# A decode block of attention and MLP: the same 2394 tasks in another issue order

## Chip, cores and metric

One core of one Trainium2 chip. The metric is device time in microseconds of one execution; medians of several executions are given.

## The reference, cut to what matters

Two layers, each an attention block over a cache and an MLP, with residuals and layer norms. Eight rows (one token each), 32 heads of 128, and the last 1024 of 4096 cached positions:

```python
W = min(4096, max(256, Sk // 4))                 # 1024
q = (layernorm(x) @ wq).reshape(B, 1, 32, 128)
scores = einsum("bhqd,bhkd->bhqk", q, k_cache[:, :, Sk - W:]) * Dh ** -0.5
x = x + softmax(scores) @ v_cache[:, :, Sk - W:] @ wo      # reshaped
x = x + gelu(layernorm(x) @ w1 + b1) @ w2 + b2
# ... the same four lines once more, with the same weights and the same cache
```

K and V of the window are 134 MB, and both layers need them. The kernel keeps part of them between a row's layers and loads 336 units of 512 KB (176 MB).

## The kernel before

The kernel builds a list of tasks and issues them in an order that a string gives. A task has an engine, a function, the tasks that it needs, and the buffers that it takes and gives back. Only legal orders pass: a task must have no unmet need, and a buffer must be free.

```python
    def emit(self):
        ...
        code, todo = iter(ORDER), list(self.tasks)
        while todo:
            k = value[next(code)]            # position in the list of tasks not yet issued
            ...
            t = todo.pop(k)
            assert not t.waits
            if t.take is not None:
                self.room[t.take] -= 1
                assert self.room[t.take] >= 0, t.take
            t.fn()
            ...
    plan = Plan({"unit": NUNIT, "s": 2, "qz": 2, "p": 1, "pv": 1, "o": 1, "ot": 2,
                 "c": 4, "C": 3, "rd": 4, "park": 2})
```

For each row and layer the 16 head pairs are cut into jobs; "7.1.8-12" is row 7, second layer, pairs 8 to 11. The tasks of a job, in order of need: *query* (PE; second layer), *expand* (DVE), *scores* (PE, one per pair; each gives its K unit back), *exponent* (ACT), *turn* (PE transposes), *place* (ACT), *totals* (PE) and *inverse* (DVE), *values* (PE, one per pair; each gives its V unit back), four *folds* and two *halves* (DVE), *gathered* (PE, two small matmuls), *finish* (DVE), and in the first layer *project* (PE) and *accrue* (DVE). When all jobs of a row's first layer are projected, its MLP runs (*sums*, *hidden*, *outer*), then its second layer's queries. A *load* (SP) takes a unit of 27.

"p" is the scratch, which exponent and folds share.

```python
    scr = state.tile([P, 512], BF16, name="scr")
    acc, parts = scr[:, 0:256].bitcast(FP32), scr[:, 256:512].rearrange("p (h d) -> p h d", h=2)
    ...
    def exponent(job):
        nc.scalar.activation(scr[:], job.s_ps[:], ACT.Exp, scale=QSCALE)    # takes "p", turn gives it back
    def fold(job, t):                                                        # takes "p", gathered gives it back
        ...
            nc.vector.scalar_tensor_tensor(out=acc, in0=o[:, t], scalar=mask[:, t:t + 1], in1=acc, ...)
```

"c" and "C" are small slots in a PSUM tile of 512 columns, c_ps.

The softmax here doesn't subtract the row's maximum and nothing guards it: scores larger than these inputs give would overflow.

Of the kernel before, what the change touches and what calls it, by code (L numbers as in the profile page):

```python
# [17 lines left out]
D = 640  # L18
H = 32
# [3 lines left out]
F = 1728  # L23
# [12 lines left out]
NOT = {}  # L36
WINDOWS = ("0:1a 0:1b 0:2a 0:2b", "1:0a 0:3a 0:3b", "1:0b 1:1a 0:4a 0:4b", "1:1b 0:5a 0:5b", "1:2a 1:2b 0:6a 0:6b",
           "1:3a 1:3b 0:7a 0:7b", "1:4a 1:4b", "1:5a 1:5b 1:6a 1:7a 1:6b 1:7b")
WINDOWS = [[(int(w[0]), int(w[2]), ord(w[3]) - 97) for w in x.split()] for x in WINDOWS]
WPOS = (("w1", -1), ("w2", -1), ("wo", 8))  # L40
NHC = 13
HALF = F - NHC * P
ORDER = (
    "I))%(z<&2/,@/-%)%9yxyxyxyxyx2.z*z,z,z,y`y`y`z),,(4y[%yZyZyZ)zIy[y[yYyZyZyZyZyZyYyY&-(y[y[y]z9/&yTyT)+*(&(yRyqy"
    "RypyRyRyRyRyRyRyjyj&yVyXyVyYyYyYyYyYyYyYyYyYy]y]y]y]y_y_ykykyk{.{.yWyWyZyVyTyfyf{&yYyY{8yYyU{6yMyWyWyWyWyVy[y^"
    "y[y]y]%y_yU$#yQyQ$##yNyNyNzfzfyGyHyHyHyHyJyGyIyKz]yKz[z[yHyGzY#yFyFyFyFyFyFyF#z^yFyF$yMyDyDyDzVzgyDzHzH%yCzQzF"
    "%yByBzCzCzZyDyBzIzWzW#ziyAyAz>z>z>z>yAyAyAz`#z:y@y@y@zHz<$yAz8z9zCz3zRzBy?z2##z4y>z3z3z3y>z2z1z.z0z6y>#-&$z+yN"
    "z;z/z:z-yNy:z,y:yLyLy~&6)#z#z#z#z#z#z)y6yzy}y`y|/y5y}y~y~y5#y|yuyuyzyzyzyYy4yByUyUyByBysyryryr+yRypyRyq,##yOy2"
    "y2y2y;y;y0y1y9#%$#&y,yXy,y,y,y,y+y<y<yVy<y+y/y/y-yHyHy+yGy7#$#y*y*y2yDyGy*y*yBy*yXy*y&y)y,y,y>yjy,y)y+y+y)y*y8"
    "y8y8yIyIyIy8y]yHy*y*y*y3y/y*y(y)y)y0#%%##y#y,y,##y4y4y4y4y*y*x|y)x}y(x|y<y<y.y&y#$y$zVy$y6x~y&x}y3x~y$y$y$y/x~"  # L50
    "zJzJzJy#y#y,y#y#y#y#x}x~x~x~z?%y$zLx}x|##x|xzxzxzx}z4xzxzz2z?xzxzxzxzz;z.xzxzxzxz##z4xyxyxxz1xxz#xxz?x~y}y}$xx"
    "z)xwyzxwxwyxyxyxyxz1xyxwyzz.#y{xvxvxvxvyqxvyp#ys#&yoxsylynxsxvyvyvxvxsxsxt2$yfyoxnxqxqxqxqy&%y_y_y_y_y_$&#%yZ%"
    "#&y]xzxiyXxiyXxxxxxiyUyUyUyUy2yTyTxiy/y/xvxvxjxu%)yKxh-+xfxfxdy%y?y>x~y=xmxm$%xkx{x{y1y1y1xcxcxcxcxcxhxfxcxqxc"
    "y+yHxpxpxe#xdy)xdy($+xjxjxxxj$x~xwxaxa#xfy3y3xwx`x_x_%xcx^x^xqxazbxlx`x^x_xlxlxlx_x_x_x_x_zUxxxgx_x^xezP##&xb("
    "xcxYxmxWy#xZxXx_#xhxTxgx]x]x]x]x]x]xYxY#xoxoxoxo%x]xXx^x[xjxjx]x]x]x[z6xSxW#%xWz1xUxVxVxVxV#xZx]xTxTxTz%yrxWxX"
    "ypy}%#z0xRxQxQxQxQxQxTxMxPyrxPydz#xPxPxPxPxP#y`yixO#y[ytxNxNxNxNxNxNyVyVyVxNxKyZxM#yfyRyRyRyRyTxLxPySyPxLyQyZ$"
    "yYxNyOxKygygygxKyU#yLxK#xIxIyHyHyHyHyHyL#>&.$xDxDxDxDyCyAxGyAy>yJxGxDxDxEy7y7xE&yBxDxDy6y?y6y6y67y5y5xUxCy7xTx"
    "ky1y5y5*#&xQy,y/x@x@-+x|x|-#xzx<y$y$y$y$xJxJxJxJx|xwxxx_x_#x;&xrxyxYxsx;x;x;xUxoxVxUxpx;xCxCx7xexBx:x:*xMxMx?x"
    "9x9$####xYx4x4x6x3x1x@x4x4x4x2x3x;x;x;xOx;x3x3xzx3x3x3x3xHx6xtx5x3x4x4x3xVxBxBxBx;xRxRxRxRx3x3x3x>x3x3x3##)x9x"
    ";x0x:$xC#x6z,x-x5x?x?#x4x1x2xKxKxK#x,x0x0x0x0x0x4x/%x3x3x.x2ynx2x.x*x:%x9x,x8&yex7x-x-x&x,x,x2yKx+x+x+yHyHx+yj"  # L60
    "x+x-x-x+x,yBx/x*x*x*x*x*x*yIy;x*x*y9yE#yU###x%y4x%y>yNx%#yLx&x&x*yIx$x$x$x$x$y*y*y2$y)y)y)y)x(y,y(y(x#x&y%%w~w"
    "~x#w~x~x~x~x~y,x~x~x~y)w~-<9y%w{w{$wzwzxu,wy*xxwxwywywywywywywyxoxixgxhxhx/xjx/x/x/x/9wwxd##$x]x`x`wqx_zsx_x)x"
    "^x;wsxSzmzm)#$)%$wmw|wmzdwozcwmwmxNwmwmwmxMx,wuwuxA)#$wjxExGxG$wiwixqwiwiwiwkwywkwlwlwlwlwix9wvwsx7wux6x,wgx2w"
    "jwjwjwgwgxWwowox+whwhx:x+x-wgwgwgx%x###wfw|x#wgwgwuw|wuwgx?wzwzwzwzx#wgw~w~wyx6w}wvwgwfwv##*+wbwbwb#wq##)wnwnw"
    "nw^w^w]w]wgy<w]wdw]w`wtw]yVwa#y4#wbwbwZwawawkwkwkwkw^yHw`y(y(w`w`w`w`w^w_#w]y=wbw]w]w`w]w_wbw^wYw[w[w^xoxow[xn"
    "y-w]%y+wZ#y:xlwYwYwYwYxhw[xew[x{wYwYwbwYxa#y*x`x`x`x`x`x`$xawWwXx_wXwWx]wWx[x[xYwYxbwW#xWxWxWxWxWwWwVxhxZ###%3"
    "wQwQxNwQxQxOxMxZwQxNwQwQxVwSwSwQwRwRwRwRwRxDxD#xAxAxAxAxAxFxAx=wcwcxBx>xBxBx;wQ&wPw`w`w`)w_w_(3#0&$x<x2x;x1x,x"
    "-x/x/#wkx-x-x-wHwEwiwix)wgwgwUwUx(wGwHwHwHwGwG#(#%wKwywZwCwCwCwCwCwFwTwTwTwGwjwAwBwEwOwBwBwCw{wLwCwKwCwCwCwHw_"
    "wCwG+wRwWyMwGwGwBwBwBwD-wKwQwQwQwKwCwCwCwCwCwCw[w[$wZwZ&##*$w?w:wDwF#y?wAw;wC$#w7wJwJw9wIx}x}x}w=w>w>w>w>wF#w="
    "w=wAw=wAwAwAw;w?w<wHxkxkwH&w;()w:w6w9w9w3w8w8w7xlw7xkw;w;w7w:w7w6w2w4w4#w4w4w4w6w4w4xjw3w3w3w3w5w3w4w3xRxDx`w3"  # L70
    "w1xrw2w2x[x@w2xKxX#xWw1w1w2w1w1w1w1w1#%x5x5#w.xIw.w.x1w0x8w.xSx/x/x/x/x/x/x1w/w/x/w.#x-x-x+w-$#x)x)w+x(w+x&x;x"
    "+#w*w*xHx#x#x(x%w-w,w*#w{w}w(x,w)x+w{w(w($.%+x#w#wkwkw|w#w#w#wowowowowowmwn*$,()#w/w/wfwjwjwGwGw/wfqq#wcwCwCpw"
    "`w`w`w`w`w+w+$#w<w<nw(w(oow7wSwMoow#w#&w2vnnnwHnw-w-wE(#pw=lolnnlmmw9#(#rrrw3w5##hw2hhwDwDhhhhkkw*hvwQw(hiwNwN"
    "h%&&ueoeeow.eneew*w*nhejkll#ettiw1w1#rhhhegggcekkehdhh#c#oooeeeebjjbb_%#x+]]cccf]bb]]]#_wx_[#wuwuZZx(ZZZZ$#wmw"
    "mwmwzZZ^wj$]wiwiwrWWZWYWwlYwyWWw`whWXwf#w]w]w]w]w]VVV#)XwVwewZwXTTTTwUwRTTwRwRwRTwNwPwPwNwOwSTTTT%$$$$#)wD__MM"
    "MwBwBOO)Lw>MMUmw6UUw7UUMMwDMMMM(#$a^^w)JKw(w*w*]]u[KqrvvsuuZZw%ZKmppMKnLLL%###%DDw*MM#ZcccDDD]%CCCEGCDREESSSEE"
    "x1EB````OMDDDDKKKKJCGRRRDQGGGwq%#EBKKJDCCCCECDABDDBCA##$wW>>>>>wRwcwR@@wP>>>w[w[>wLwY###wI<wT<wHwHwH##::99wW:;"
    "wH$wSw?w?w?w?wE8w>w>88#7w<w:777w9788w6w6w68w:8888%)#)wvw*w+w+w+w+%/#)w&^^[[AA000r22(o;1/l08j0wV0-wU555FF/////]"
    "A[[[[00RRW0Q#(##$PPPO999LL#$&`$))F&((0CB0A0(((<(((99#)*&))333))))</--9...-)$($&(>(#&&&#88%%%@?F%J%%2E;(:1%#$$-"
    "-;$$$$$-$3#0&(++%+#*)$##$#")  # L80


class Job:
# [59 lines left out]
def _kernel(ctx: ExitStack, tc: tile.TileContext, A_small, A_k, A_v, A_wq, A_wo, B_w1, B_w2, out):  # L143
# [46 lines left out]
    xn = single["yT"]  # L190
# [67 lines left out]
    def narrow(n, nb, name):  # L258
        if nb == 1:
            return single[name]  # L260
        return units[free.pop()][:, 0:n * nb].rearrange("p (f b) -> p f b", b=nb)
# [464 lines left out]
    rows = []  # L726
    for b in range(NB):
        at, h = {}, (held | set(ALSO.get(b, ()))) - set(NOT.get(b, ()))
# [58 lines left out]
                         after=[d for d, h0, h1 in ends if h0 < h + 2 and h1 > h] + [head], take="park" if h == 0 else None)  # L787
            head = head or t

    jobs = rows[0][0]["s"] + rows[0][0]["k"]  # L790
    for b in range(NB):
        for layer, row, k in WINDOWS[b]:
            jobs = jobs + [rows[row][layer]["s"][k]]
        jobs = jobs + [job for job in rows[b][1]["k"] if any((w, i) not in job.held for w in "kv" for i in range(job.i0, job.i1))]
        jobs = jobs + (rows[b + 1][0]["k"] if b + 1 < NB else [])
# [7 lines left out]
    extra = {}  # L803
    for name, pos in WPOS:
        if pos < 0:
# [5 lines left out]
    def part0(job, last):  # L811
        def tail(done, h0, h1):
            projects(job, done, h0, h1, CHAIN, h1 == 2 * job.i1)
        add_job(job, (), 0, tail=tail if last else False)

    def part1(job, last, early, rank0, ask=None):
        job.ends = []
        done = add_job(job, early, rank0, ask=ask, tail=(lambda *x: job.ends.append(x)) if last else False)
        if not last:
            job.ends.append((done, 2 * job.i0, 2 * job.i1))  # L820

    for job in rows[0][0]["s"]:
        part0(job, False)
    for job in rows[0][0]["k"]:
        part0(job, job is rows[0][0]["k"][-1])
    for b in range(NB):
        ask = chain(b, projected[b] + asked + [weights["w1"], weights["w2"]])
        asked.clear()
        ahead = rows[b + 1][0]["k"] if b + 1 < NB else [rows[r][i]["s"][k] for i, r, k in WINDOWS[b]]
        base = min(t.pos for x in ahead for t in x.loads.values())  # L830
# [4 lines left out]
        for job in rows[b][1]["s"]:  # L835
            job.stored = ask(job, base, True)
        for layer, row, k in WINDOWS[b]:
            job = rows[row][layer]["s"][k]
            if layer == 0:
                part0(job, False)  # L840
            else:
                if b + 1 == NB:
                    job.direct = asked[:1]
                part1(job, b + 1 == NB and (layer, row, k) == WINDOWS[b][-1], [job.stored], 0)
        if b + 1 < NB:
# [11 lines left out]
    y8 = narrow(NKC, NB, "y8")  # L857
# [43 lines left out]
```

## Time and profile before

| | before |
|---|---|
| median (3 runs) | 490.17 us (490.11 to 490.87) |
| span of the profiled run | 488.7 us |
| PE / DVE / ACT busy | 80% / 52% / 16% |
| bytes moved | 192.20 MB |
| plateau of the loads | 416 to 420 GB/s |
| last landing, then first step of the last MLP, then end | 469.0, 478.1, 488.7 us |

The prediction below shows the lines. They are read in this order: the DMA and GB/s rows say that the stream of loads is full nearly everywhere (DMA at 9 in 37 of 40 slices, 416 to 420 GB/s in most); the stretches say where it isn't; the chain says what ends last.

### The profile page before, as it was taken

Reading aid. Unit: us, or ns where it says so; the run is one execution under the profiler, and the core shown is the slowest. Engines: PE = TensorE matmul, PEld = TensorE weight load, DVE = VectorE, ACT = ScalarE, POOL = GpSimd, SP = SyncE. Lnnn points to the kernel's source line nnn. Section 1 sums busy time; section 2 is a strip of 40 time slices with the busy share of each in tenths; the row PEclk is TensorE's granted clock in tenths of the full one; section 3 lists DMA queues with packets and bytes.
Section 4 is the critical chain, followed back from the end, with each engine's and each line's share of the span. In section 5 each row is a group of like instructions: output and inputs, shape, how many; then the busy total and the mean of one; then the engine's idle time right before and its main releaser. Section 6 shows DMA issues by size and latency. Waiting matters only on the chain.

```text
span 488.7 us, 16784 instructions
## 1 busy us (share of the span) xinstructions
PE 392.6 (80%) x7201; PEld 212.3 (43%) x7201; DVE 256.2 (52%) x1116; ACT 76.4 (16%) x195; POOL 12.7 (3%) x24
## 2 busy tenths in 40 slices
PE   1412645998899998898989989988999899889985
PEld 0300124553365436542564355535552464365354
DVE  3001422455735764477454755666466746757563
ACT  1000000111211111112111211112112111121220
POOL 1000000000000000000000000000000000000001
PEclk9996555556655755557555575587556655765765
DMA  8999999999999999999999999999999999999920
GB/s 328 417 420 420 438 421 417 418 417 418 416 418 415 416 416 420 402 411 419 418 380 403 417 417 411 412 419 414 416 416 417 418 373 392 416 415 414 417 91 4
DMA packets 49898, 192.20 MB, mean 393 GB/s; under 512 B 5792, under 2 KB 5792, under 8 KB 48800
## 3 DMA queue, kind: packets, MB, share of 16 engines
q1 hardware_dynamic: 49824, 191.13, 96.5%
q8 instruction: 56, 0.92, 0.7%
q14 instruction: 18, 0.15, 0.1%
HBM read 191.10 MB, written 0.01 MB: 391 GB/s over the span
## 4 chain that ended last, share of the span: by engine, by line
PE 53%; DMA 21%; DVE 17%; issue 4%; ACT 3%; POOLq 0%; ACTq 0%; SPq 0%; DVEq 0%
PE s_ps L435 13%; PE o_ps L476 12%; DMA unit<-in_A_k_dram 9%; PE c_ps L536 6%; PE c_ps L698 6%; DMA unit<-in_A_v_dram 6%; DVE scr L486 5%; DMA wo_sb<-in_A_wo_dram 4%; PE c_ps L450 3%; PE c_ps L319 3%; PE o_ps L511 2%; PE c_ps L359 2%; PE c_ps L500 2%; DVE scr L484 2%; PE c_ps L273 1%
## 5 line engine op out<-in xcount | busy, mean ns | idle before, releaser
L435 PE MATMUL s_ps<-unit,low 128*1 128x512 bf16 (+3 forms) x1024 | 123.5, 564 | 18.9 <-DMA unit<-in_A_k_dram 13.2
L476 PE MATMUL o_ps<-unit,misc 128*8 128x512 bf16 (+3 forms) x888 | 108.2, 555 | 12.9 <-DMA unit<-in_A_v_dram 6.8
L444 ACT ACTIVATE scr<-s_ps 128x512 bf16<-128x512 f32 x80 | 47.8, 597 | 217.7 <-PE c_ps L500 127.9
L486 DVE SCALAR_TENSOR_TENSOR scr<-o_ps,low,scr 128x128 f32<-128x128 f32 x213 | 74.1, 348 | 5.9
L484 DVE TENSOR_SCALAR scr<-o_ps,low 128x128 f32<-128x128 f32 x71 | 24.7, 348 | 46.7 <-PE c_ps L450 30.1
L536 PEld LDWEIGHTS <-wo_sb 128*128 128x128 bf16 x1280 | 38.4, 103 | 21.5 <-issue 14.3
L435 PEld LDWEIGHTS <-low 128*1 128x1 bf16 (+3 forms) x1024 | 22.6, 91 | 50.3 <-issue 34.8
L698 PEld LDWEIGHTS <-wq_sb 128*128 128x128 bf16 x1280 | 38.0, 102 | 13.4 <-issue 12.6
L698 PE MATMUL c_ps<-low,wq_sb 128*128 128x1 bf16 x1280 | 40.8, 165 | 0.8 <-ACT misc L454 0.4
L454 ACT CAST misc<-c_ps 128x48 bf16<-128x48 f32 (+2 forms) x80 | 21.8, 272 | 123.0 <-DVE misc L465 22.1
L476 PEld LDWEIGHTS <-misc 128*8 128x8 bf16 (+3 forms) x888 | 20.2, 91 | 38.6 <-issue 27.1
L450 PEld LDWEIGHTS <-scr 128*128 128x128 bf16 x320 | 15.1, 104 | 39.9 <-ACT scr L444 35.7
L500 PEld LDWEIGHTS <-scr 128*128 128x128 bf16 x142 | 11.7, 105 | 39.1 <-DVE scr L495 12.2
L450 PE MATMUL c_ps<-misc,scr 128*128 128x16 bf16 x320 | 21.1, 176 | 8.7 <-ACT scr L444 5.7
L536 PE MATMUL c_ps<-misc,wo_sb 128*128 128x1 bf16 x630 | 19.8, 165 | 7.5 <-DMA wo_sb<-in_A_wo_dram 5.1
L465 DVE TENSOR_REDUCE misc<-c_ps 128x8 f32<-128x64 f32 (+2 forms) x80 | 16.0, 200 | 17.9 <-PE c_ps L460 11.6
L319 PEld LDWEIGHTS <-w_sb 128*128 128x128 bf16 x675 | 20.4, 104 | 9.9 <-issue 9.4
L460 PE MATMUL c_ps<-misc,low 128*128 128x48 bf16 (+2 forms) x80 | 16.5, 206 | 9.8 <-ACT misc L454 7.0
L500 PE MATMUL c_ps<-low,scr 128*128 128x8 bf16 x142 | 17.5, 176 | 7.6 <-DVE scr L493 3.3
L427 DVE CAST low<-c_ps 128x6 bf16<-128x6 f32 (+2 forms) x56 | 8.5, 154 | 28.0 <-ACT misc L454 16.9
L536 PE MATMUL c_ps<-low,wo_sb 128*128 128x1 bf16 x650 | 20.9, 165 | 2.3 <-DVE misc L465 1.4
L495 DVE TENSOR_TENSOR scr<-scr 128x128 bf16<-128x128 f32 x71 | 20.3, 286 | 2.4 <-PE s_ps L435 0.2
(98 smaller groups left out, 305.4 us busy)
## 6 DMA issues: line engine op xcount, KB each, us to landing
unit<-in_A_v_dram SPq DMA_DIRECT2D x168, 512.0 KB, 9.2
unit<-in_A_k_dram SPq DMA_DIRECT2D x168, 512.0 KB, 9.0
wq_sb<-in_A_wq_dram SPq DMA_DIRECT2D x5, 1024.0 KB, 8.9
wo_sb<-in_A_wo_dram SPq DMA_DIRECT2D x1, 5120.0 KB, 21.3
w_sb<-in_B_w_dram SPq DMA_DIRECT2D x1, 2176.0 KB, 25.1
w_sb<-in_B_w_dram SPq DMA_DIRECT2D x1, 2160.0 KB, 29.0
unit<-in_A_small_dram SPq DMA_DIRECT2D x1, 15.0 KB, 1.7
out_dram<-unit SPq DMA_DIRECT2D x1, 10.0 KB, 1.4
```

Of the source, the lines that this page charges most:

```text
L319: nc.tensor.matmul(t["h", k][1][:, fc - halves[k][0], :], lhsT=w_sb[:, kc * F + c0:kc * F + c0 + P], rhs=t["y"][:, kc, :], start=(kc == 0) ...
L435: nc.tensor.matmul(job.s_ps[32 * a:32 * a + r + 1, :], lhsT=view(low, job.qz + 5 + d - (d + 1) * r, (d + 1, r + 1)), rhs=k[:, 512 * a:512 ...
L444: nc.scalar.activation(scr[:], job.s_ps[:], ACT.Exp, scale=QSCALE)
L450: nc.tensor.matmul(job.t_ps[1][:, c], lhsT=scr[:, c * P:(c + 1) * P], rhs=small_ident.rearrange("p (a r) -> p a r", a=4), start=True, stop ...
L454: nc.scalar.copy(view(misc, 0, (64, job.n), (1, 4), (4, 4)), job.t_ps[1][:, :, :, 0:job.n].rearrange("p t a i -> p i a t"))
L476: nc.tensor.matmul(job.o_ps[32 * g:32 * g + 4 * r + 4, :], lhsT=view(misc, 48 * r + g, (4, 4 * r + 4)), rhs=v[:, 512 * g:512 * g + 512], s ...
L484: nc.vector.tensor_scalar(out=acc, in0=o[:, 0], scalar1=mask[:, 0:1], scalar2=None, op0=ALU.mult)
L486: nc.vector.scalar_tensor_tensor(out=acc, in0=o[:, t], scalar=mask[:, t:t + 1], in1=acc, op0=ALU.mult, op1=ALU.add)
L495: nc.vector.tensor_tensor(out=parts[:, 1], in0=acc, in1=parts[:, 0], op=ALU.subtract)
L500: nc.tensor.matmul(job.o8[1], lhsT=parts[:, h], rhs=sel, start=(h == 0), stop=(h == 1))
L536: nc.tensor.matmul(sums[1][:, n:n + 1], lhsT=wo_sb[:, h, n * P:(n + 1) * P], rhs=job.ot[:, h - 2 * job.i0:h - 2 * job.i0 + 1], start=(h == ...
L698: nc.tensor.matmul(job.q_ps[1][:, h - 2 * job.i0:h - 2 * job.i0 + 1], lhsT=wq_sb[:, kc, h * DH:(h + 1) * DH], rhs=xn[:, kc, :], start=(kc ...
```

## The change

The intent: a search found another order in a model of the tasks, whose task and hand-over times had been fitted to a trace of this kernel. Only the string changes (and a list that stays empty):

```diff
+EARLY = []
 ...
 ORDER = (
-    "I))%(z<&2/,@/-%)%9yxyxyxyxyx2.z*z,z,z,y`y`y`z),,(4y[%yZyZyZ)zIy[y[yYyZyZyZyZyZyYyY&-(y[y[y]z9/&yTyT)+*(&(yRyqy"
+    "%()z*z*z*z*-.z(z(z(z)%2ykyk=z/yjy~4/0.+(:&&%y`y`)5+,/yZyZyZytyjyjyjyqyjyjyj*&.-yWye++y}yUy|yUyUy_yUyUyUyUyU)y]"
 ... (36 more lines of either)
```

Decoded, the end of the loads shows what it does. The last load was a K unit and is now the V unit of the same pair:

```text
before: ... scores 7.1.0-3 i1, scores 7.1.0-3 i2, LOAD 7.1.3-5 K i4, totals 7.1.5-8, values 7.1.5-8 i5, ...
after:  ... fold 7.1.0-3 k0, fold 7.1.0-3 k1, expand 7.1.3-5, LOAD 7.1.3-5 V i4, scores 7.1.3-5 i3, i4, ...
```

## The prediction

No term of its sum is among them: 0 + 1.5 + 2.3 + 0 = 3.8 us from 490.17, or 486.4, said as 486.

- The "some seven" loads that must be out are an estimate, 9.0 and 9.2 us to landing (medians for K and V units in the profile before) over 1.25 us a unit.

> **What bounds the kernel now.** I read the page from the top (engines, slices, queues), then the chain of work, then the waits of the queue that issues loads, then tables of stretches, and last the end of the trace in order of time.
>
> ```profile
> span 488.7 us, 16784 instructions
> PE 392.6 (80%) x7201; PEld 212.3 (43%) x7201; DVE 256.2 (52%) x1116; ACT 76.4 (16%) x195; POOL 12.7 (3%) x24
> ...
> DMA  8999999999999999999999999999999999999920
> GB/s 328 417 420 420 438 421 417 418 417 418 416 418 415 416 416 420 402 411 419 418 380 403 417 417 411 412 419 414 416 416 417 418 373 392 416 415 414 417 91 4
> DMA packets 49898, 192.20 MB, mean 393 GB/s; under 512 B 5792, under 2 KB 5792, under 8 KB 48800
> ```
>
> The DMA row is 9 in 37 of the 40 slices, and the rate stays on a plateau of 416 to 420 GB/s in most of them. PE is busy 80% over the span but is never the row that is full everywhere. So the bound is the stream of loads, for all but the ends. I take 418 GB/s for the plateau. 192.2 MB at 418 GB/s is 459.8 us.
>
> Three things stand between 459.8 us and the span of 488.7 us: a slow start, dips of the stream, and the tail. These stretches size them (columns: stretch, its length, busy time of PE, weight loads, DVE, ACT and POOL with counts, granted PE clock, DMA share, GB/s):
>
> ```profile
> 0.00:10.00 10.00, 1.09 (x4) 0.71 (x4) 3.98 (x29) 1.28 (x1) 2.36 (x7) 1.00 0.79 305
> 190.00:200.00 10.00, 9.04 (x166) 5.27 (x166) 4.30 (x22) 1.49 (x5) 0.54 (x1) 0.50 1.03 413
> 200.00:210.00 10.00, 9.03 (x153) 4.82 (x154) 5.92 (x27) 1.26 (x4) 0.54 (x1) 0.50 1.02 404
> 240.00:250.00 10.00, 8.97 (x227) 6.76 (x224) 3.55 (x19) 1.71 (x5) 0.54 (x1) 0.50 1.01 400
> 250.00:260.00 10.00, 8.91 (x175) 5.31 (x172) 5.80 (x31) 0.39 (x2) 0.54 (x1) 0.50 1.01 385
> 260.00:270.00 10.00, 9.59 (x150) 4.07 (x151) 4.96 (x22) 2.22 (x5) 0.00 (x0) 0.50 1.02 402
> 300.00:310.00 10.00, 9.29 (x176) 5.17 (x174) 6.34 (x33) 1.25 (x4) 0.54 (x1) 0.50 1.02 402
> 390.00:400.00 10.00, 9.26 (x200) 5.95 (x196) 3.18 (x21) 1.28 (x5) 0.54 (x1) 0.50 1.01 391
> 400.00:410.00 10.00, 9.47 (x203) 6.03 (x207) 5.75 (x29) 1.53 (x4) 0.54 (x1) 0.50 1.00 372
> 410.00:420.00 10.00, 9.07 (x137) 3.71 (x135) 7.92 (x27) 2.37 (x6) 0.00 (x0) 0.67 1.02 408
> 458.20:469.00 10.80, 8.83 (x115) 3.20 (x114) 7.53 (x35) 2.51 (x7) 0.00 (x0) 0.82 0.83 337
> 469.00:478.10 9.10, 7.97 (x218) 6.32 (x217) 4.24 (x23) 1.51 (x4) 0.00 (x0) 0.50 0.01 4
> 478.10:488.70 10.60, 4.95 (x145) 4.55 (x145) 4.12 (x22) 0.41 (x2) 1.64 (x1) 0.50 0.01 3
> ```
>
> The reader is to see: the first 10 us lose (418 - 305)/418 x 10 = 2.7 us. The nine stretches between 190 and 420 us lose, by the same rule, 0.1 + 0.3 + 0.4 + 0.8 + 0.4 + 0.4 + 0.6 + 1.1 + 0.2 = 4.3 us; the others lose next to nothing. In the stretch of the last load 337 GB/s x 10.8 us is 3.64 MB, which takes 8.7 us at the plateau, so the last byte came at about 466.9 us. Check: 459.8 + 2.7 + 4.3 = 466.8. What remains is 2.1 us from the last byte to its being usable, 9.1 us until the last projection is done, and 10.6 us of the last MLP.
>
> The end of the chain of waits (start, length, what):
>
> ```profile
> 458.18 10.84 DMA unit<-in_A_k_dram
> 469.02 0.04 issue
> 469.06 0.60 PE s_ps L435 x4
> ...
> 475.17 0.99 PE o_ps L511 x32
> 476.16 0.81 PE park L760 x30
> 476.98 0.04 PE c_ps L500 x2
> 477.02 1.09 PE park L760 x40
> ```
>
> The last load to land is a K unit, so a whole attention step follows it: scores, exponent, turn, totals, values, finish, and the output projection on L760.
>
> [...]the load queue waited 75.8 us in 82 waits for score matmuls and 58.3 us in 64 for value matmuls, the tasks that free a unit. So a load goes out when PE frees its buffer, and PE's order shapes the stream.[...]
>
> **The change part by part.** Nothing is removed or added in work: the empty list EARLY changes nothing, and the windows, kept units and parked units are as before. The order string is a list of picks from the list of tasks not yet issued. I decoded both strings by that rule, without building or timing anything. Both hold the same 2394 tasks: 943 on PE, 904 on DVE, 192 on ACT, 339 load issues. 187 of the 943 PE tasks keep their place among PE's, 84 of 339 loads among the loads, 112 of 192 on ACT; the mean shift on PE is 3.8 places. Bytes, matmuls and evictions are unchanged, so 392.6 us of PE busy and 459.8 us of stream should both be found again.
>
> *Start.* The first loads come in another order, but the stream is full from 10 us on in either. Gain 0.
>
> *Steady part.* For each unit that PE consumes I counted how many later loads could already have been issued at that point of PE's order. The smallest is 6 almost everywhere in both, and the means for loads 40 to 280 go from 12.4, 11.4, 11.9, 11.4 to 12.6, 11.6, 12.2, 11.2: nearly the same reserve. A load takes about 9 us to land (the page's issue table) and a unit 1.25 us of the plateau, so some seven must be out to keep it full. The dips sit where PE works on MLP and query matmuls, which free no unit. The order can at best win the 4.3 us; I give it a third, by judgement, as the reserve hardly changes: 1.5 us.
>
> *Tail.* This I can see. Before, 27 PE tasks stand from the first use of the last load to the end of the searched part. In the new order the last load is the V unit of the same job, and only 8 stand there: one column step, six gathers of two heads and one small gather. Six gathers are 60 matmuls, from the row of 30 in 0.95 us: 1.9 us; with the column step at about 0.5 us and the small one at 0.2 us this is 2.6 us, and with hand-overs some 3.5 us against 9.1. But PE must then do the rest earlier, and between 458.2 and 469.0 it was idle only 10.8 - 8.8 = 2.0 us. So not 5.6 us. In both orders the last load's buffer is freed by the same score task (row 7, pair 11). Weighting the PE tasks behind that by the trace's durations, 22.8 us remain in the new order against 23.7. Before, the 19.9 us from that release to 478.1 held 8.8 + 8.0 = 16.8 us of PE and 3.1 us of idle. New: 16.8 - 0.9 = 15.9 us and perhaps 1.7 us of idle, an estimate, so 17.6 us: a gain of 2.3 us.
>
> *Last MLP.* Outside the searched order: 10.6 us stay.
>
> Sum: 0 + 1.5 + 2.3 + 0 = 3.8 us from 490.17, or 486.4; I say 486.
>
> **The rivals.** *The search fits its model and not the chip.* Then the gain stays on paper: a task issued too early waits at the head of PE's or DVE's queue and the stream dips elsewhere. For it: the reserve is no larger in the middle, and for loads 280 to 320 the count of consumers with a reserve below 6 rises from 3 to 6. Against it: the times were fitted to a trace. This gives 488 to 493.
>
> *The stream becomes full and the tail gets all it can.* Gains of 4.3 and of 5.5 us would end at 480.4. For it: the model knows hand-overs now. Against it: PE is 89 to 95% busy in the dips, so there is little room to move work. This is the only way to 2%.
>
> *The tail is hidden anyway.* If the last release comes at the same time and PE is the bound there, moving the gathers ahead merely delays the last values; the last landing stays at 469 and only the 0.9 us comes: 488 to 489.
>
> **Range and chances.** The middle of the three is 486; low 481.5 is nearly the whole ceiling of some 10 us, high 490.5 is no gain. Faster by 2% means below 480.4, above that ceiling: 0.05. Slower by 2% would need 500, that is more than twice today's dips: 0.02. Within 2%: 0.93.
>
> **What would show it.** The same 192.2 MB and a plateau of 418; dips between 190 and 420 us that sum to about 3 us; the last load a V unit that lands at 466 to 468; from landing to the first step of the last MLP 5 to 8 us instead of 9.1; then 10.6 us as before. Wrong would be: a plateau other than 418, a start that dips in the first 100 us, more than 6 us of dips, or a tail of more than 9 us.

## More of the kernel before

```python
    c_bank = psC.tile([P, 512], FP32, name="c_ps")
    ...
    qo = c_bank[:, 0:NB * H].rearrange("p (b h) -> p b h", b=NB)
    slots[:] = [c_bank[:, k:k + 16] for k in range(448, 512, 16)]          # "c": 4
    large[:] = [c_bank[:, k:k + 64] for k in range(NB * H, 448, 64)]       # "C": 3
```

Turn, totals, gathered, query, project and the MLP on PE write slots of it; inverse, expand, finish and accrue on DVE and place and store on ACT read them.

## The result, and the profile after

| | before | after |
|---|---|---|
| median, same rounds | 490.14 us (489.93 to 490.87, 4 runs) | 493.01 us (492.72 to 494.0, 4 runs) |
| ratio of after to before | | 1.0059, 95% interval 1.0041 to 1.0077 |
| span of the profiled run | 488.7 | 491.0 |

A ratio is the mean time of one kernel's fast runs over the mean of the other's of the same rounds, so not quite the ratio of the medians. The change is within the 2% class, 2.9 us slower, and outside the predicted range. The granted clock is no rival: runs of the kernel before at a clock of 0.622 and of 0.715 took 489.91 and 490.15 us. The page of the changed kernel:

```profile
span 491.0 us, 16801 instructions
...
PE 386.1 (79%) x7201; PEld 214.1 (44%) x7201; DVE 258.5 (53%) x1116; ACT 76.4 (16%) x195; POOL 12.7 (3%) x24
...
GB/s 322 418 420 419 448 411 418 419 415 417 419 416 411 418 416 417 408 410 417 417 403 388 419 416 416 418 415 415 418 411 415 419 396 358 416 415 401 402 50 4
DMA packets 49898, 192.20 MB, mean 391 GB/s; under 512 B 5792, under 2 KB 5792, under 8 KB 48800
```

The bytes, the matmuls and the plateau are the same (192.20 MB, 7201, and 415 to 420 GB/s in 25 of 40 slices). The two slices before the last of the stream (401, 402) were 414 and 417 before. Stretches of the changed kernel (stretch, length, busy time of PE, weight loads, DVE, ACT, POOL with counts, granted clock, DMA share, GB/s):

```profile
400.00:410.00 10.00, 9.22 (x195) 5.88 (x195) 5.92 (x29) 1.15 (x4) 0.54 (x1) 0.50 0.98 358
410.00:420.00 10.00, 8.76 (x149) 3.99 (x145) 7.82 (x29) 2.65 (x6) 0.00 (x0) 0.85 1.00 384
...
450.00:460.00 10.00, 9.74 (x150) 4.04 (x150) 6.69 (x26) 2.19 (x5) 0.00 (x0) 0.63 0.99 380
459.00:469.81 10.81, 9.56 (x137) 3.77 (x137) 7.85 (x33) 2.51 (x7) 0.00 (x0) 0.74 0.85 342
469.81:480.40 10.59, 8.86 (x228) 6.45 (x224) 5.35 (x27) 1.52 (x4) 0.00 (x0) 0.50 0.01 3
480.40:491.00 10.60, 4.96 (x145) 4.56 (x145) 4.12 (x22) 0.41 (x2) 1.65 (x1) 0.50 0.02 3
```

The dips in the prediction's nine stretches between 190 and 420 us sum to 4.1 us, against 4.4 before, both unrounded (the prediction adds rounded terms to 4.3). From 450 to 460 us the rate is 380, where it was 417: a new dip of 0.9 us. From the last landing (469.81) to the first step of the last MLP it takes 10.6 us, against 9.1; the last MLP takes the same 10.6.

The end of the chain that ended last (start, length, what) no longer runs through a load:

```profile
466.03 0.61 ACT scr L445
466.68 0.29 PE c_ps L451 x4
467.00 0.36 DVE scr L485
467.38 0.36 DVE scr L487
467.77 0.36 DVE scr L487
468.16 0.36 DVE scr L487
468.56 1.48 PE o_ps L477 x9
```

Before, a load of 10.84 us stood here, from 458.18 to 469.02. Now it is exponent, turn, four folds, values, and so on: the chain of the one scratch.

**Where the 2.3 us of the two spans come from.** PE's, DVE's and ACT's instructions were matched one by one with the tasks of the list (the counts agree), which gives every task's start and end in both traces. The marks along the end:

| mark | before | after | later by |
|---|---|---|---|
| statistics of row 6's MLP | 394.19 | 395.03 | 0.84 |
| statistics after row 6's MLP | 403.53 | 404.00 | 0.47 |
| load 300 / load 324 landed (counted from 0, by landing) | 423.58 / 454.35 | 424.34 / 454.39 | 0.76 / 0.04 |
| statistics of row 7's MLP | 435.36 | 437.29 | 1.93 |
| row 7's first exponent of the second layer (7.1.12-16) | 449.98 | 452.19 | 2.21 |
| score task that frees the last load's unit (7.1.8-12 i11) ends | 455.02 | 457.08 | 2.06 |
| last load landed | 469.02 | 469.81 | 0.79 |
| last projection done | 478.09 | 480.35 | 2.26 |

So the loads land about when they did until 454 us, and the tasks of the last two rows are already 2 us behind. One execution is a weak witness: two_rooms_old (below), which has the old order, has row 7's statistics at 434.26 and not at 435.36 us. But the lag recurs: in five traces whose order is the new one unaltered up to that mark it is reached at 437.29 to 438.21, in eight with the old order in row 6 at 434.05 to 435.94.

The stretch between the statistics of rows 6 and 7, before and then after:

```profile
394.19:435.36 41.17, 37.35 (x736) 21.12 (x732) 26.09 (x109) 7.71 (x20) 1.08 (x2) 0.62 1.01 397
```

```profile
395.03:437.29 42.26, 37.52 (x756) 21.97 (x756) 27.07 (x115) 7.80 (x20) 1.08 (x2) 0.66 1.01 394
```

It is 1.1 us longer: 20 more matmuls and six more DVE instructions stand in it, and PE is idle 4.7 us instead of 3.8. So work put ahead of row 7's statistics is a rival to the waits. row6_new (below), with the same order up to there, has 42.67 us with 38.44 busy, so this split is not stable. From the score task to the last projection little changes. The stretch of before (columns as above):

```profile
455.02:478.09 23.07, 19.80 (x413) 11.72 (x410) 14.05 (x65) 4.62 (x12) 0.00 (x0) 0.71 0.53 216
```

and of the changed kernel:

```profile
457.08:480.35 23.27, 20.09 (x380) 10.64 (x375) 15.03 (x62) 4.62 (x12) 0.00 (x0) 0.65 0.48 194
```

One trace has its own error here: in both traces some loads land 0.9 to 1.3 us late though the DMA row stands at 9. Before, loads 119, 167, 211, 257 and 301 (counted from 0, by landing) landed at 192.2, 253.5, 309.9, 368.8 and 425.9 us, each 2.2 to 2.5 us after the one ahead of it, where the median from the 100th to the 300th is 1.24 us; after, six loads from the 68th to the 292nd came 2.1 to 2.3 us after the one ahead, with a median of 1.23. Their cause was not shown. It is not always the same load (load 119 landed 0.98 us earlier in the changed kernel than before, load 139 again within 0.08 us). So marks are compared within a trace or against landings.

### The profile page after: what moved, and what is told of

It is laid out like the page before. It is cut to its first block, busy times and chain, and to the rows that moved or that the text cites. A ratio compares the mean times of both kernels' runs of the same rounds, so it can differ in the third digit from the quotient of the medians.

```text
span 491.0 us, 16801 instructions
## 1 busy us (share of the span) xinstructions
PE 386.1 (79%) x7201; PEld 214.1 (44%) x7201; DVE 258.5 (53%) x1116; ACT 76.4 (16%) x195; POOL 12.7 (3%) x24
## 2 busy tenths in 40 slices
DMA packets 49898, 192.20 MB, mean 391 GB/s; under 512 B 5792, under 2 KB 5792, under 8 KB 48800
## 4 chain that ended last, share of the span: by engine, by line
PE 38%; DMA 38%; DVE 16%; issue 3%; ACT 3%; SPq 0%; POOLq 0%; DVEq 0%; ACTq 0%
DMA unit<-in_A_v_dram 21%; DMA unit<-in_A_k_dram 14%; PE o_ps L477 9%; PE s_ps L436 9%; DVE scr L487 6%; PE c_ps L699 5%; PE c_ps L537 3%; DMA wq_sb<-in_A_wq_dram 2%; PE c_ps L360 2%; PE c_ps L451 2%; PE c_ps L320 2%; DVE scr L485 2%; ACT scr L445 2%; PE o_ps L512 2%; PE c_ps L274 1%
## 5 line engine op out<-in xcount | busy, mean ns | idle before, releaser
L436 PE MATMUL s_ps<-unit,low 128*1 128x512 bf16 (+3 forms) x1024 | 118.4, 541 | 34.8 <-DMA unit<-in_A_k_dram 26.9
L699 PEld LDWEIGHTS <-wq_sb 128*128 128x128 bf16 x1280 | 38.2, 102 | 13.6 <-issue 12.7
L537 PEld LDWEIGHTS <-wo_sb 128*128 128x128 bf16 x1280 | 38.1, 101 | 12.6 <-issue 10.7
L699 PE MATMUL c_ps<-low,wq_sb 128*128 128x1 bf16 x1280 | 40.8, 165 | 1.1 <-ACT misc L455 0.6
L455 ACT CAST misc<-c_ps 128x64 bf16<-128x64 f32 (+2 forms) x80 | 21.8, 273 | 117.5 <-PE c_ps L451 17.4
L477 PEld LDWEIGHTS <-misc 128*8 128x8 bf16 (+3 forms) x888 | 22.5, 91 | 39.3 <-issue 22.9
L451 PE MATMUL c_ps<-misc,scr 128*128 128x16 bf16 x320 | 21.1, 176 | 11.6 <-ACT scr L445 8.4
L537 PE MATMUL c_ps<-misc,wo_sb 128*128 128x1 bf16 x740 | 22.9, 164 | 3.2 <-DVE misc L524 1.9
L512 PE MATMUL o_ps<-misc,unit 128*128 128x1 bf16 x544 | 18.2, 165 | 4.6 <-DVE scr L487 2.3
L404 DVE TENSOR_SCALAR park<-unit 128x512 uint32<-128x512 uint32 x32 | 21.7, 682 | 0.0
L413 DVE TENSOR_SCALAR unit<-park 128x512 uint32<-128x512 uint32 x32 | 21.1, 682 | 0.2 <-PE s_ps L436 0.2
```

The lines of the kernel that those rows point to most:

```text
L436: nc.tensor.matmul(job.s_ps[32 * a:32 * a + r + 1, :], lhsT=view(low, job.qz + 5 + d - (d + 1) * r, (d + 1, r + 1)), rhs=k[:, 512 * a:512 ...
L451: nc.tensor.matmul(job.t_ps[1][:, c], lhsT=scr[:, c * P:(c + 1) * P], rhs=small_ident.rearrange("p (a r) -> p a r", a=4), start=True, stop ...
L455: nc.scalar.copy(view(misc, 0, (64, job.n), (1, 4), (4, 4)), job.t_ps[1][:, :, :, 0:job.n].rearrange("p t a i -> p i a t"))
L477: nc.tensor.matmul(job.o_ps[32 * g:32 * g + 4 * r + 4, :], lhsT=view(misc, 48 * r + g, (4, 4 * r + 4)), rhs=v[:, 512 * g:512 * g + 512], s ...
L512: nc.tensor.matmul(job.o_ps[:, h:h + 1], lhsT=v[:, c * DH:(c + 1) * DH], rhs=view(misc, 64 * slot(job, i) + g + 4 * t, (1, 1)), start=(fir ...
L537: nc.tensor.matmul(sums[1][:, n:n + 1], lhsT=wo_sb[:, h, n * P:(n + 1) * P], rhs=job.ot[:, h - 2 * job.i0:h - 2 * job.i0 + 1], start=(h == ...
```

## The experiments

Eighteen kernels ran, all with correct results. Each is a legal order of the same tasks; edits are shown as lists of tasks, as the string itself says nothing to a reader. Names of theories in the quoted texts: T1, the scratch chain of the tail starts late because a small gather stands behind five score tasks; T2, row 7's work starts late; T3, the loss is made in rows 6 and 7, after 395 us; T4, any order but the old one costs 2 to 3 us; T5, most of it is made in row 6; T6, in the new tail.

### First cuts: splices whose joints did harm

**head_new_tail_old** and **head_old_tail_new**: one order up to the first statistics of row 7's MLP, the other's order of what is left.

```diff
 # head_new_tail_old                      # head_old_tail_new: the reverse
-ORDER = old
+ORDER = new up to "sums" of row 7's MLP, then the rest in old order
```

> The new order up to the first statistics matmul of row 7's MLP (about 436 us), then the old order. Theory (the 2.9 us are lost in the last 50 us, where the one scratch buffer is handed to and fro between exponents and folds, and the new order starts that chain 2.2 us later): 490 to 491, that is the kernel before plus the 0.3 us by which the new order's loads are behind at 440 us. Rival stream (the dips between 200 and 420 us, which sum to some 5 us against 4.3, set the end): 491.5 to 492.5. Rival start (the new first 100 us): 492.5 to 493.

> The complement: the old order up to the same matmul, then the new order. Theory: 492 to 493, nearly the whole loss is here. Rival stream: 490.5 to 491.5. Rival start: 490 to 490.5.

Measured: 493.26 us, ratio 1.0057 (1.0038 to 1.0077), and 492.46, ratio 1.0045 (1.0028 to 1.0061), against 490.18. Both halves seem to cost everything, which cannot be added up. The traces name the reason: at 436 us the two orders have not issued the same tasks. In the second, a turn and a score task stood ahead of the statistics, which began at 438.10 us instead of about 436.35, 1.75 us of the joint's own; in the first, new loads met the old PE order and a K unit landed 3.7 us later (440.55 against 436.90). Inconclusive.

**late_old** (new to row 6's MLP at 395 us, then old) and **row7_old** (new, but 395 to 447 us in old order):

```diff
 # late_old
+ORDER = new up to 395 us, then the rest in old order
 # row7_old
+ORDER = new up to 395 us, old from 395 to 447 us, then the rest in new order
```

> The new order up to the start of row 6's MLP (about 395 us), cut where the two orders have issued the same loads and differ by five tasks only, then the old order. Theory (last row: the new order starts the last row's chain of MLP, queries and attention later, since the last V units of row 7's first layer come two loads later, and puts four query tasks instead of two ahead of that row's score tasks; nothing before 395 us costs anything): 490.2, 489.5 to 491.0. Rival (the first 395 us cost something that the k-th landing, equal within 1 us in both traces, hides): 492 or more. Rival (any order other than the old one costs 2 to 3 us, whatever is changed, since the old one was picked among many on the chip): 492 to 493.5.

> The new order, with the tasks between the start of row 6's MLP and row 7's second layer norm (395 to 447 us) put in the old order, loads included; the tail after 447 us stays new. Theory: the first layer norm of row 7 comes at 436.8 instead of 438.7 us, the second at 446.6 instead of 447.7, the end 1.1 us earlier: 491.9, 491.3 to 492.4. Rival (only the tail counts): 493.0. Rival (any new order costs): 492.5 to 493.5.

Measured: 493.21, ratio 1.0052 (1.0032 to 1.0073), and 493.6, ratio 1.0059 (1.0045 to 1.0074), against 490.7. Again the joint: row 6's statistics started at 396.59 us against 394.19 and 395.03, as a projection and DVE tasks had come ahead of them, a unit was freed late, and the loads were 2.0 us behind from the 288th on. Inconclusive for what they should have told apart.

### Hand edits of the new order

**gather_early**: the small gather, and the finish that the hand-over seemed to need, moved forward.

```diff
 # gather_early, PE                         # DVE
-query h24, h16, h28, h20, 5 score tasks, gathered 5.1.3-5
+query h24, h16, h28, h20, gathered 5.1.3-5, 5 score tasks
 # DVE
-folds 5.1.3-5, halves 5.1.3-5, ..., finish 6.1.5-8
+finish 6.1.5-8, folds 5.1.3-5, halves 5.1.3-5, ...
```

> The new order with two tasks moved: the small gather of row 5, pairs 3 to 4, goes ahead of five score tasks on PE, right behind the query matmuls before it, and the finish task of row 6, pairs 5 to 7, goes ahead of the folds on DVE to free the small PSUM slot that the gather takes. Theory: the exponent behind the gather starts at about 450.0 instead of 452.19 us, and the end follows it: 491.0 (490.7 to 491.5). Rival stream in the tail (loads issued late after 450 us set the end, since their units are freed by the score tasks, which this moves back by only 0.2 us): 492.7 to 493.3.

Measured: 495.37, ratio 1.0107 (1.0085 to 1.0128): slower than the new order. The waits of DVE from 446 to 456 us:

```profile
DVE c_ps L524 <- PE c_ps L699: 1.6, 1, 1.6
```

L524 is finish, L699 query. The moved finish of job 6.1.5-8 waited 1.6 us for a query of row 7, with which it shares no data: only the tile c_ps. The folds behind it were 2.3 us late. So the gather came at 451.70 us, hardly earlier than in the new order (451.94), but now held up the five score tasks behind it: the first exponent began at 454.54 instead of 452.19. I read this line only as a local accident then; it is the first of three such waits (below).

**queries_back** and **row7_old_queries_back**: two of four queries moved behind the scores and the gather, in the new order and in row7_old.

```diff
 # queries_back, PE
-query 7.1.12-16 h24, query 7.1.8-12 h16, query 7.1.12-16 h28, query 7.1.8-12 h20, 5 score tasks, gathered 5.1.3-5
+query 7.1.12-16 h24, h28, 5 score tasks, gathered 5.1.3-5, query 7.1.8-12 h16, h20
 # DVE, moved with them
-expand 7.1.8-12, restore k0, inverse 5.1.0-3, finish 6.1.5-8
+inverse 5.1.0-3, finish 6.1.5-8, expand 7.1.8-12, restore k0
```

> The new order, with two query tasks of the last row (heads 16 to 23) moved behind the five score tasks and the small gather that follow them on PE, as the old order has it. The five score tasks free five units, so five loads go out 1.07 us earlier (40 matmuls at 0.53 us per 20), and the first exponent of the last row starts at 451.1 instead of 452.19. Theory: 492.0, 491.4 to 492.5. Rival (the tail is set by the last landing or by PE's total work, which do not change): 492.8 to 493.2.

> Both of these edits on the new order. Theory, the two adding up: 490.9, 490.2 to 491.5. Rival (only one of the two counts): 491.8 to 492.3. Rival (any new order costs): 492.5 to 493.5.

Measured: 494.82, ratio 1.0081 (1.0064 to 1.0098), and 494.86, ratio 1.0084 (1.0069 to 1.0099). Both expectations failed: T1 and T2 as they stood would have gained 1 to 2 us. None of the three mends gained: gather_early is clearly slower than the new order, and these two lean that way, with intervals that overlap its own (1.0041 to 1.0077). The two DVE tasks that went along were not tested apart.

**two_rooms_new**: the folds and halves of the last six jobs work in columns of the query weights (`wq_sb`) that are no longer needed, so exponent and folds no longer share the scratch there.

```diff
+    acc2, parts2 = wq_sb[:, 1, 24 * DH:24 * DH + 256].bitcast(FP32), ...
+    def room(job):
+        late = job.layer == 1 and (job.b > 5) and (job.b == 7 or job.i0 < 5)
+        return (acc2, parts2) if late else (acc, parts)
     def fold(job, t):
+        acc, parts = room(job)            # the same in halve and gathered
```

> The new order, nothing moved, but the folds and halves of the last six jobs use columns of the query weights that are no longer needed instead of the scratch buffer of the exponents. So exponents and folds no longer wait for each other in the tail. Theory: each of five rounds of the tail saves an exponent and its hand-over, some 0.6 us each; 489.5 to 491.5. Rival PE order (the turns and gathers keep their place on PE, so nothing starts earlier): 492.5 to 493.3. Rival stream: 492.5 to 493.3 as well.

Measured: 492.18, ratio 1.0037 (1.0021 to 1.0053), against 1.0059 (1.0041 to 1.0077) of the new order in other rounds, intervals that overlap a little. From the last landing to the last projection the trace has 8.4 us against 10.5: 2.2 us less, of which 1.0 us was given back by a later last landing (470.82). From the score task that frees the last load's unit to the last projection it has 21.16 us against 23.27. The scratch is part of the new tail's bound.

### Clean joints

At task 1332 (297 us) the two orders have issued the same loads and PE tasks, and at 1678 (357 us) all the same but three DVE tasks.

```diff
 # half_new_old
+ORDER = new up to 297 us, then the rest in old order
 # three_quarters_new_old
+ORDER = new up to 357 us, then the rest in old order
 # queries_front_old: the old order, PE
-query 7.1.12-16 h24, h28, 5 score tasks, gathered 5.1.3-5, query 7.1.8-12 h16, h20
+query 7.1.12-16 h24, query 7.1.8-12 h16, query 7.1.12-16 h28, query 7.1.8-12 h20, 5 score tasks, gathered 5.1.3-5
 # two_rooms_old: the old order with the edit of two_rooms_new
```

> The new order up to task 1332 (about 297 us, in row 4's MLP), then the old one. At this cut the two orders have issued the same tasks but for one on DVE and none that is a load or on PE, so the joint makes no artefact. Theory T3 (the loss is made in rows 6 and 7, after 395 us; the first 400 us cost nothing since each load lands when it did before): the same as before, ratio 0.999 to 1.001, that is within 0.5 us of it, and the last landing within 0.3 us of 469.0. Rival T4 (anything but the old order costs 2 to 3 us wherever it differs): ratio 1.004 to 1.006.

> The same with the cut at task 1678 (about 357 us), where the two sets differ by three DVE tasks, two of them ones that the new order does 14 us later. T3: as before within 0.5 us (ratio 0.999 to 1.001). T4: 1.004 to 1.006. If this one loses and the cut at 297 us does not, the loss is made by what the new order does between, or by the three DVE tasks of the joint.

> The old order with one thing of the new one: the two query tasks h16 and h20 of row 7's job 8-12 stand ahead of the five score tasks and the small gather at 447 us, as in the new order, and not behind them. T3 in its local form (what stands ahead of the scores and of the gather is what costs): two queries are 1.2 us of PE, so the row's first exponent starts 1 to 1.3 us later, and the load freed by the score task too; total +0.7 to +1.7 us, ratio 1.0015 to 1.0035. Rival (the place of these two doesn't matter, as moving them back in the new order did not help): within 0.3 us, ratio under 1.0007. A third way, as with the other hand edits: +2 to +3 us.

> The old order, and the folds and halves of the last six jobs work in free columns of the projection weights' buffer and not in the scratch that the exponents write. In the new order this shortened the time from the last landing to the last step by 2.2 us and gained 0.8 us. If the chain over the one scratch bounds the old order's tail too: 488.3 to 489.5 us (ratio 0.996 to 0.9985), better than both. If the old tail is bound by PE's work behind the last release: within 0.3 us.

| run | median | ratio to before (491.07) |
|---|---|---|
| half_new_old | 490.27 | 0.9989 (0.9966 to 1.0011) |
| three_quarters_new_old | 490.93 | 1.0005 (0.9985 to 1.0024) |
| queries_front_old | 492.0 | 1.0021 (1.0001 to 1.0041) |
| two_rooms_old | 490.08 | 0.9986 (0.9967 to 1.0005) |

The first two settle the place: 1678 tasks of the new order cost nothing that these rounds can see (the interval ends at 0.24%, or 1.2 us), so T4 falls and the loss is made after 357 us. The third puts a size on one local thing: two query tasks ahead of scores and gather cost 1.0 us in the old order, and its trace has row 7's first exponent at 451.14 us, 1.2 later than in three_quarters_new_old (449.95), as expected. Taking the same two tasks away from the new order did not help (queries_back): a cost that can be added cannot always be taken away elsewhere. The fourth leans to a gain of 0.7 us, within its interval of none. In its trace the stretch from the score task that frees the last load's unit to the last projection is hardly shorter than before (23.07):

```profile
454.09:476.70 22.61, 19.31 (x410) 11.44 (x410) 13.96 (x65) 4.61 (x12) 0.00 (x0) 0.72 0.55 221
```

### Row 6 against row 7

```diff
 # row6_old
+ORDER = new to 357 us, old from there to row 7's MLP (443 us), then the rest in new order
 # row6_new
+ORDER = new to 443 us, then the rest in old order
 # row6_mended: the new order; left of the bar now stands ahead of what is right of it
+DVE: inverse, finish 7.0.5-8 | finish 4.1.0-3, expand 5.1.0-3, inverse 6.1.8-12      (were behind those three)
+DVE: halve 6.1.8-12 k1 | parking of 7.0.5-8;  halve 6.1.5-8 k1 | finish 6.1.8-12, inverse 6.1.5-8
+PE:  turn 7.0.8-12 | query 6.1.0-3 h4;        gathered 6.1.5-8 | totals 7.0.8-12
 # half_two_rooms: half_new_old with the edit of two_rooms_new
```

> The new order to 357 us (shown harmless), the old order through row 6 and row 7's MLP up to the gating at 443 us, then the new order with its tail. Theory T5 (most of the loss is made in row 6, where DVE and PE tasks put ahead of the hand-overs of the scratch chain delay row 7's MLP by 1.9 us; row 7's new order and tail cost only 0.4 us): +0.2 to +0.9 us on before, ratio 1.0005 to 1.002. Rival T6 (the new tail alone costs what the splice at 436 us showed): ratio 1.004 to 1.005.

> The complement: the new order to the turn of job 5.1.3-5 at 443 us, then the old order with its tail; at this joint four tasks differ, one load and one score task among them, both earlier. T5: +1.5 to +2.2 us on before, ratio 1.003 to 1.0045, and row 7's first root 1.9 us later than before against the landings. T6: within 0.5 us of before.

> The new order with four hand-overs of row 6 mended: inverse and finish 7.0.5-8 ahead of three other DVE tasks (in the trace PE's turn 6.1.5-8 waited 0.97 us for this finish); halve 6.1.8-12 k1 ahead of the parking of 7.0.5-8 (0.7 us); turn 7.0.8-12 ahead of query h4 (0.4 us); halve 6.1.5-8 k1 ahead of two DVE tasks and its gather ahead of the totals (0.5 us). T5: row 7's MLP starts 1 to 1.8 us earlier and the whole is 1 to 1.8 us below the new order, ratio to before 1.001 to 1.0035. Rival (as all hand edits of the new order so far): 1.005 or more, another hand-over taking the place of those.

> The new order to 297 us, then the old one, and the folds of the last six jobs in their own columns: the two things that did not cost (0.9989 and 0.9986) in one kernel. If the second scratch shortens the tail whatever comes before: ratio 0.998 to 0.999, 0.5 to 1 us below before. If neither is more than chance: 0.9995 to 1.0005.

| run | median | ratio to before (491.1) |
|---|---|---|
| row6_old | 492.38 | 1.0032 (1.0013 to 1.0052) |
| row6_new | 493.75 | 1.0062 (1.0039 to 1.0086) |
| row6_mended | 493.07 | 1.0047 (1.0029 to 1.0065) |
| half_two_rooms | 489.18 | 0.9972 (0.9953 to 0.9991) |

Row 6 in new order with the old tail costs 0.6%, row 7 with the new tail after an old row 6 costs 0.3%, and both together 0.6%. So T5 is right that row 6 alone makes the loss, though it costs more than T5's 1.5 to 2.2 us. The joint of row6_new did no visible harm: from row 7's first statistics (437.83) to the freeing score task (457.58) it takes 19.75 us, against 19.67 before and 19.79 after. On row 7, put at 0.4 us, T5's number failed with 1.6 us, but here a joint did harm again. In row6_old the statistics of row 7 start at 435.56 us, as before, and the freeing score task ends at 456.83, as late as after. Of this delay 1.0 us arises at the joint at 443 us: a score task that the new order has ahead of it anyway (6.1.0-3 i0) came between the old MLP's tasks, and the MLP's outer product began at 443.35 instead of 442.25 us. So the cost of row 7's new order by itself is not shown.

**row6_mended** teaches most. In the new order PE's turn of job 6.1.5-8 waits 0.97 us. The list of what happened (start, length, engine, line, operation, idle time before and its releaser), changed kernel:

```profile
420.17 0.21 DVE L466 TENSOR_REDUCE misc<-c_ps 128x8 f32<-128x64 f32 x1
...
420.53 0.16 DVE L466 TENSOR_REDUCE misc<-c_ps 128x6 f32<-128x48 f32 x1
...
420.95 0.16 DVE L524 TENSOR_TENSOR misc<-c_ps,misc 128x6 bf16<-128x6 f32 x1
421.17 0.24 PE L451 MATMUL c_ps<-misc,scr 128*128 128x16 bf16 x4 [0.97 <-DVE misc L524]
```

From this I took finish 7.0.5-8 for the cause and moved it ahead of three DVE tasks, inverse 6.1.8-12 among them. With row6_mended:

```profile
420.58 0.16 DVE L524 TENSOR_TENSOR misc<-c_ps,misc 128x6 bf16<-128x6 f32 x1
...
421.06 0.22 DVE L466 TENSOR_REDUCE misc<-c_ps 128x8 f32<-128x64 f32 x1
...
421.33 0.24 PE L451 MATMUL c_ps<-misc,scr 128*128 128x16 bf16 x4 [0.89 <-DVE misc L466]
```

Finish is 0.4 us earlier, and the turn is not (421.33; in row6_new, whose head is the new order unchanged, it is at 421.28). It now waits for the reduce of another job, 6.1.8-12, which the edit had put last. The statistics of row 7 came at 438.01, against 437.83 in row6_new. So T5's expectation of 1 to 1.8 us failed. The ratio is 1.0047 against the new order's 1.0059 of other rounds, with intervals that overlap; I name no cause for that.

**half_two_rooms** is the one version whose interval lies below the kernel before: 489.18, 0.28% under before with an interval of 0.09 to 0.47%. Its two parts alone gave 0.11 and 0.14%, and neither was clear of none. What makes it so is open: from the last landing to the last projection it has 8.9 us (467.59 to 476.45) against 9.1 before, 0.2 of the 1.4. The second scratch is not seen to do anything there: half_new_old, with one scratch, has 8.9 us too (467.71 to 476.58), and its profiled run took 489.02 us against 488.92. One interval of eighteen can lie below 1 by chance, and this one was not repeated.

### The last two

**row6_mended2** puts both tasks that the turn waited for ahead of a restore, puts the restore and two others (finish 4.1.0-3 and expand 5.1.0-3) behind the folds and halves, and moves a gather forward. **row6_old_two_rooms** is row6_old with the second scratch.

```diff
 # row6_mended2: the new order, DVE
-restore wv k1, finish 4.1.0-3, expand 5.1.0-3, inverse 6.1.8-12, inverse and finish 7.0.5-8, folds 6.1.8-12, halve k0, parking, halve k1
+inverse 7.0.5-8, inverse 6.1.8-12, finish 7.0.5-8, folds and halves 6.1.8-12, restore wv k1, finish 4.1.0-3, expand 5.1.0-3, parking
 # PE
-values 6.1.5-8 i5, query 6.1.0-3 h0, totals 6.1.5-8, gathered 6.1.8-12
+gathered 6.1.8-12, values 6.1.5-8 i5, totals 6.1.5-8, query 6.1.0-3 h0
 # and the other two of row6_mended
```

> The new order, row 6 mended more fully than before: both tasks for which the turn 6.1.5-8 waited stand ahead of the second restore, the restore and two other DVE tasks stand behind the folds and halves, the small gather stands ahead of the values and the query behind it, and the two mends from before. If the chain is what the delay is made of: the turn at 420.3 to 420.6 against 421.3 (relative to landings as before), the exponent of 7.0.8-12 1 us earlier or more, row 7's first statistics at 436.3 to 437.0, and the time 0.7 to 1.5 us below the new order: ratio 1.003 to 1.0045. If yet another wait takes its place further on: the turn earlier but row 7's statistics within 0.3 us of the new order's and the ratio 1.005 to 1.006.

> row6_old (1.0032) with the second room for the folds of the last six jobs. If the one scratch is what the new tail loses by: ratio 0.998 to 1.0002, that is 1.5 to 2.5 us less than row6_old, and from the last landing to the last step under 9 us. If the new tail is bound by something else: 1.002 to 1.0035, at most 0.5 us better.

| run | median | ratio to before (490.3) |
|---|---|---|
| row6_mended2 | 495.35 (4 runs) | 1.0099 (1.0079 to 1.012) |
| row6_old_two_rooms | 490.42 | 0.9997 (0.9979 to 1.0015) |

row6_old_two_rooms did what was expected: the 0.32% of row6_old is gone (its interval was 0.13 to 0.52%, now -0.21 to 0.15%). The stretch table from the score task that frees the last load's unit to the last projection, first of row6_old:

```profile
456.83:479.81 22.98, 17.93 (x380) 10.63 (x375) 15.23 (x63) 4.63 (x12) 0.00 (x0) 0.79 0.51 205
```

and then of row6_old_two_rooms:

```profile
456.98:478.29 21.31, 17.42 (x382) 10.61 (x375) 15.02 (x63) 4.50 (x12) 0.00 (x0) 0.81 0.54 219
```

1.7 us less for the same tasks and the same order, with PE busy as long (17.9 and 17.4). So the one scratch bounds the new tail. It does not make it longer than the old one (22.98 us against 23.07): row 7 still comes late here (the score task ends at 456.98), and the second scratch makes up for it with a shorter tail. The old tail is not bound so: a second scratch left it at 22.61 us against 23.07 (two_rooms_old), and at 22.81 against 22.82 (half_two_rooms, half_new_old). The last landing to the last projection is 8.8 us here, as expected under 9.

row6_mended2 is the slowest of all. Its turn came when expected (420.35, no wait), and its folds at 420.66 instead of 421.59 us in row6_new. Then this stands in the waits of PE from 416 to 438 us:

```profile
PE c_ps L537 <- DVE low L428: 3.2, 1, 3.2
```

and in the list:

```profile
423.62 0.17 DVE L428 CAST low<-c_ps 128x6 bf16<-128x6 f32 x1
423.83 0.94 PE L537 MATMUL c_ps<-misc,wo_sb 128*128 128x1 bf16 x30 [3.23 <-DVE low L428]
```

L428 is expand 5.1.0-3, one of the two that I had moved behind the folds as harmless; L537 is project 7.0.5-8, another row and another layer. They share only the tile c_ps. ACT's store behind it waited 5.0 us for this projection, and the gather that should have been early came at 425.66.

### What ties the failed mends together

Three times a task of one engine waited for a task of another on c_ps with which it has no data in common: gather_early (finish for query, 1.6 us), row6_mended (turn for an inverse, 0.89 us), row6_mended2 (project for expand, 3.23 us). Each time the releaser was the last task that stood earlier in the list, on another engine, and touched that tile. The slots differ each time too. So it was counted over whole traces: for each task on PE, DVE and ACT that touches c_ps in the searched part, the start of its first instruction there against the end of all earlier listed instructions of each other engine on c_ps, whatever their slot. Before there are 1742 such pairs and after 1747. In none does the later task start before the earlier ones have ended. As a control, the PE tasks that do not touch c_ps (scores, values, columns and the gathers of two heads) started before the earlier listed DVE users of it had ended in 178 of 528 cases before and in 159 of 528 after. Nor is every tile bound as a whole: on the SBUF tile `misc`, counted the same way, the later listed task started before an earlier one of another engine had ended in 218 of 1715 pairs before and 214 of 1722 after.

So in these kernels c_ps is one buffer for three engines, and the order of the list binds them to each other through it, without an exception in 3489 pairs (1742 before, 1747 after). What keeps this order was not shown. The plan counts seven slots of it and has no such term; its only limits are needs, counted buffers and the order within an engine. That the search's model lacked it too is a conclusion from the plan; the model itself I have not seen.

How much of the loss it makes was not shown by a run. PE's idle times ahead of a c_ps task that, by the trace, a c_ps task of another job ended sum to 11.6 us before and 12.6 us after over the searched part, and to 3.9 and 3.4 us from 357 us on, where the loss is made. So this sum does not show the loss. The three waits above stand in hand-edited orders; the new order itself has one of the kind, the 0.97 us of turn 6.1.5-8 for finish 7.0.5-8, of 1.9 us by which row 7's statistics are late. That c_ps makes the loss is not shown. No run split c_ps, so what that would do to these waits is not shown either.

## Why the prediction was wrong, point by point

**Start: right.** It predicted no gain; the 40th landing came at 89.57 us, 0.15 earlier.

**Steady stream: too large.** It predicted a gain of 1.5 us. (A reading there is off by a point, without effect: PE is up to 96% busy in the dips, not 95.) The nine stretches went from 4.4 to 4.1 us of dips, and 450 to 460 us lost 0.9 us that it had not lost. Loads landed about when they did before until 454 us.

**Tail: this step failed.** It said that from the release of the last load's unit to the last projection 17.6 us would remain instead of 19.9. Three terms of it were wrong. It kept the time of the release, "freed by the same score task", as it was; that task ended 2.06 us later (457.08 against 455.02). It took the issue of the load at 458.2 for the release, though the score task had ended 3.2 us before it. And it took PE's work for what fills the stretch, with 0.9 us less of it; PE was busy 20.09 us instead of 19.80, and the stretch was 23.27 instead of 23.07. So there was no gain of 2.3 us but a loss of 0.2, behind a release that was 2.1 late. What bounds the new tail is the chain over the one scratch: a second one took 1.7 us out of it in row6_old_two_rooms and 2.1 in two_rooms_new (23.27 to 21.16), with the orders unchanged. So the shorter tail that was predicted was there to be had, but behind a wait that the prediction did not count.

**The last byte: misread.** It put the last byte at 466.9 us, from bytes at the plateau, and 2.1 us from there to its being usable. In the trace the stream thins out, with 238, 90, 66 and 33 GB/s in the half microseconds from 466.5 us on, and the last packet ended at 468.6 us, 0.4 before the landing (0.3 in the trace after).

**What it did not look at: whether rows 6 and 7 arrive in time.** It counted loads per unit and PE tasks behind the last load. The delay comes before: row 6 in new order costs 3.0 us with the old tail (row6_new), and the whole new order 2.9. (Row 7 and the new tail after an old row 6 cost 1.6, of which 1.0 is the joint's.) That it arises in the hand-overs between PE, DVE and ACT is argued from the traces, as no mend took it away.

**Last MLP: right**, 10.6 us in both. Bytes and plateau: right.

**The rivals.** The first, that the search fits its model and not the chip, came nearest: the time lies in its range of 488 to 493 but for the last hundredth, and the hand edits show its mechanism ("a task issued too early waits at the head of PE's or DVE's queue") at work (3.23 us on PE in row6_mended2, 1.6 us on DVE in gather_early), though not how much of the loss it is. Its signs were weighed too lightly, as "the times were fitted to a trace": times can be right while the dependencies are not complete (whether they were in that model was not seen). Its addition that "the stream dips elsewhere" fits the 380 GB/s from 450 to 460 us. The third, a tail that is hidden anyway, fell, as the tail became longer.

**Shown by runs:** the place (after 357 us); that row 6 in new order makes the loss by itself; that the one scratch bounds the new tail and not the old one; a cost of 1.0 us for two queries put ahead, at the edge of its interval. **Shown by traces alone:** that c_ps orders three engines as one buffer. **Open:** what row 6's 3.0 us are made of, waits on c_ps, other hand-overs or work put ahead, as both mends made new waits; what row 7's new order costs by itself; and whether half_two_rooms wins by more than chance.

## What to carry to other kernels

Before trusting a searched order, check in a trace that every wait in it is in the model, and look for waits between tasks that share no data; in these kernels a PSUM tile cut into seven slots behaved as one buffer for three engines (0 of 3489 pairs changed their order). Where a small buffer is shared by two stages (here exponent and folds), test a second one: here it was worth 1.7 to 2.1 us of the new tail, and at most 0.5 of the old. When two orders are spliced to find a loss, cut where both have issued the same tasks, and check the trace at the joint before believing the time.
